# Last batch of an attention and gated-FFN kernel: gates in seven products of quarters, and three token pairs by turns

## The chip, the cores and the metric

The kernel runs on one core of one Trainium2 chip. The metric is the device time of one execution in microseconds (us). An execution uses TensorE (PE, matrix products; PEld is its weight load), VectorE (DVE), ScalarE (ACT), GpSimd (POOL) and the queue of SyncE (SP) that issues most DMAs. Before the change the median of three runs is 321.75 us (321.69 to 322.04). A difference under 0.2% (0.64 us) can't be told from no change.

## The reference

Two stages follow each other. The first is attention in which a query sees only the keys that have the same nearest centroid; the second is a gated feed-forward network without biases.

```python
# q, k, v: (4 batches, 8 heads, 768 tokens, 64), centroids: (8, 16, 64)
q_assign = argmax(normalised(q) @ normalised(centroids).T)     # per token, of 16
k_assign = argmax(normalised(k) @ normalised(centroids).T)
scores = where(q_assign == k_assign, q @ k.T / 8, -1e9)
attn = softmax(scores) @ v
x = attn as (3072 tokens, 512)
gate = 1 / (1 + exp(-(x @ w_gate)))                            # w_gate: 512 x 1536
val = x @ w_val                                                # w_val:  512 x 1536
out = (gate * val) @ w_out                                     # w_out: 1536 x 512
```

## The kernel before

The four batches are worked through one after the other, each with 96 steps of attention (8 heads of 12 half steps). A step is one `do_scores` (a matmul of 128 keys by 384 queries into a PSUM bank, then an exp on ScalarE into `es`) and, two steps later, one `do_av` (three small matmuls that gather `es` times v). When a head pair is done, `normalise` (L367) divides on VectorE and GpSimd, and `turn_x` (L939) sends the result through a transposing DMA on SP into `xTb`, the FFN's input: 4 chunks `dc` of 128 features by 768 tokens. The steps are numbered through all batches; the last batch has steps 288 to 383. The lists `bg`, `at` and `SCHED` say at which step a piece of side work (loads, splits, sums) is issued. Each engine carries out its own instructions in the order in which this program issues them; the program's order is written out by hand.

The FFN of a batch is a queue of short pieces ("atoms"), from which `ffn_run` (L846) takes some in every step, so that TensorE always has work between the scores. An FFN batch has two blocks of 384 tokens (three tiles of 128). For each block and each of 12 columns blocks `fc` of 128 hidden features there is a gate atom (four matmuls over `dc` into one bank, then a tanh on ScalarE) and a val atom (four matmuls into one bank, then one VectorE instruction, (tanh + 1) times val into the fp16 tile `hT`). The sigmoid is had from the tanh, with the factors 1/2 put elsewhere.

The output product `hT` by `w_out` goes over pairs of token tiles. From batch 1 on a pair takes seven products of half size rather than eight (the Strassen-Winograd scheme): `Sums.make` (L724) forms four sums of quarters of `hT` on VectorE, sums of quarters of `w_out` were formed once (T1 to T4), each of the seven products is six matmuls of 256 columns, and additions on VectorE put the quarters of the result together. The pairs are tiles (0,1), (3,2) and (4,5).

In the last batch block 0 is put into the queue at step 379.5, behind what is left of the batch before; its atoms come up after the last `do_av` and follow each other without anything between. Block 1 comes behind it. In block 1 the atoms of pair (0,1) (list `aside`) and half products of pair (3,2) alternate with the gate and val atoms; what is left of (3,2) and all of (4,5) comes last (`closing`, L576). PSUM has eight banks: four in `ring` (scores, gates, vals, some outputs), two in `avp` (attention) and two in `op` (outputs).

Of the kernel before, what the change touches and what calls it, by code (L numbers as in the profile page):

```python
# [95 lines left out]
}  # L96


# [1 line left out]
def kernel(  # L100
# [294 lines left out]
    T = {}  # L395
# [102 lines left out]
    def tok(b, t, f):  # L498
        return HB[b, t // 3][:, HF * f : HF * f + HF, bass.ts(t % 3, 128)]

    def store(src, b, c0, n, m=slice(0, DM)):
        def f():
            SP.dma_start(
                out=out[b * S : (b + 1) * S].rearrange("(p c) m -> p c m", c=NCH)[
                    :, c0 : c0 + n, m
                ],
                in_=src,
            )
# [7 lines left out]
    def ffn_atoms(xT, t0, n, b, final=False):  # L516
# [5 lines left out]
        when = SUMS_LAST if final else SUMS_AT[b >= PB, blk]  # L522

        def gate(fc, st):
            def f():
                need(("w", fc // WQ, 0), *(("x", b, p, t0 // 128 + c) for p in range(NP) for c in range(n // 128)))
                if fc == 0:
                    HB[b, blk] = htp.tile([128, NFC, 384], HP, name="hT")
                g = bank(512, name="g")
                for dc in range(NDC):  # L530
                    PE.matmul(  # L531
                        out=g[:, 0:n], lhsT=wg[fc // WQ][:, dc, fc % WQ, :],
                        rhs=xT[:, dc, t0 : t0 + n],
                        start=(dc == 0), stop=(dc == NDC - 1),
                    )
                th = thp.tile([128, 384], FP, name="th")
                ACT.activation(th[:, 0:n], g[:, 0:n], AF.Tanh)  # L537
                st.append(th)

            return f  # L540

        def val(fc, st):
            def f():
                need(("w", fc // WQ, 1))
                w = bank(512, name="v")
                for dc in range(NDC):
                    PE.matmul(  # L547
                        out=w[:, 0:n], lhsT=wv[fc // WQ][:, dc, fc % WQ, :],
                        rhs=xT[:, dc, t0 : t0 + n],
                        start=(dc == 0), stop=(dc == NDC - 1),  # L550
                    )
                DVE.scalar_tensor_tensor(  # L552
                    HB[b, blk][:, fc, 0:n], st[0][:, 0:n], 1.0, w[:, 0:n], ALU.add, ALU.mult
                )
# [17 lines left out]
        if final:  # L572
            return closing(b, gv, sm[(3, 2)], sm[(4, 5)])
        return gv + outs

    def closing(b, gv, ma, mb):  # L576

        ac, order = [], []  # L580
        plus = lambda dst, a, z: DVE.tensor_tensor(dst, a, z, ALU.add)

        def pair(m, bk):
            st = {}
# [7 lines left out]
            def mm(o, k, g, n, start, a=0, z=HD):  # L592
                w = lhs[k]()
                for c in range(g, g + n):
                    PE.matmul(  # L595
                        out=o, lhsT=w[:, c, :], rhs=rhs[k][:, c, a:z],
                        start=start and c == 0, stop=c == HF - 1, skip_group_check=True,
                    )

            def product(k, g=0, n=HF):  # L600
                def f():
                    z = {1: "a", 4: "d", 6: "x", 7: "x", 5: "y", 3: "y"}[k]
                    if g == 0 and k in (1, 4, 6, 5):
                        if k == 1:
                            st["ob"] = osp.tile([128, 2, DM], FP, name="ob")
                        st[z] = bk(z)
                    o = st[z][:, 0:HD]
                    mm(o, k, g, n, k not in (7, 3))
                    if g + n < HF:
                        return  # L610
                    if k == 1:
                        ACT.activation(C(0, 0), o, AF.Copy)
                    elif k == 4:
                        plus(C(1, 0), o, C(0, 0))
                    elif k == 6:
                        plus(C(0, 1), o, C(0, 0))
                    elif k == 5:
                        plus(C(1, 1), o, C(0, 0))
                    elif k == 7:
                        plus(C(1, 0), o, C(1, 0))  # L620
                        plus(C(1, 1), o, C(1, 1))
                        store(st["ob"][:, 1:2], b, m.t2, 1)
                    else:
# [4 lines left out]

            def last(parts):
                def f():  # L630
                    for a, z in parts:
                        o = bank(z - a, name="o_end")
                        mm(o, 2, 0, HF, True, a, z)
                        plus(st["ob"][:, 0, a:z], o, st["ob"][:, 0, a:z])
                    store(st["ob"][:, 0:1, 0:HD], b, m.t1, 1, slice(0, HD))

                return f

            return product, last

        two = {}

        def bank_a(z):
            if z in "ad":
                need(*(("wo", i) for i in range(WOP)), *(("wt", i, c) for i in range(4) for c in range(2)))
                two[z] = out_bank()
            return two[{"x": "a", "y": "d"}.get(z, z)]

        pa, la = pair(ma, bank_a)
        pb, lb = pair(mb, lambda z: bank(512, name="o_end"))  # L650
        early = [pa(k, g, HF // 2) for k in (1, 4, 6, 5) for g in (0, HF // 2)]

        def drained(f):
            def g():
                while aside:
                    aside.pop(0)[1]()
                f()

            return g

        early[0] = drained(early[0])
        atoms = gv[:14]
        for i, x in enumerate(gv[14:]):
            atoms.append(x)
            if i < len(early):
                atoms.append((0.0, early[i]))
        for f in (
            pa(7), pb(1), pb(4), pa(3), pb(6), pb(5), la([(0, HD)]), pb(7), pb(3),
            lb([(0, HD // 2), (HD // 2, HD)]),
        ):  # L670
            atoms.append((0.0, f))
        return atoms

    def plain_out(b, blk, t):
        OA = SCHED.get(f"oa{b}{384 * blk}", SCHED.get("oa", 4))
# [33 lines left out]
        },  # L709
    }  # L710

    SUMS_LAST = {
# [3 lines left out]
    }  # L716

    class Sums:


        def __init__(self, b, t1, t2):
            self.b, self.t1, self.t2, self.of = b, t1, t2, {}

        def make(self, i, c0=0, c1=HF):  # L724
# [3 lines left out]
            if c0 == 0:  # L728
                if i == 4 and c1 == HF:
                    self.of[4] = self.of[2]  # L730
                elif i == 4:
                    self.of[4] = tp.tile([128, 12, 128], HP, tag="T", name="T")[:, 0:HF]
                else:
                    self.of[i] = sump.tile([128, HF, 128], HP, tag="sum", name="sum")
            o = self.of[i][:, c]
            if i == 1:
                DVE.tensor_tensor(o, a2(0), a2(1), ALU.add)
            elif i == 2:
                DVE.tensor_tensor(o, self.of[1][:, c], a1(0), ALU.subtract)
            elif i == 3:  # L740
                DVE.tensor_tensor(o, a1(0), a2(0), ALU.subtract)
            else:
                DVE.tensor_tensor(o, a1(1), self.of[2][:, c], ALU.subtract)

    def product_out(b, sums):

# [783 lines left out]
    for b in range(B):  # L1530
        xT = xtp.tile([128, NDC, S], HP, tag="xTb", name="xTb")
        key = min(b, 1)
        for i in range(2 if b else NPT):
            u = BASE[b] + (DONE0[i] if b == 0 else 96 - 12 * halved(b) if i == 0 else 96)
            lag = SCHED.get(f"lag{key}{i}", 8)
            if b == B - 1 and i:
                break
# [54 lines left out]
```

## Time and profile before

| | |
|---|---|
| median of the runs | 321.75 us |
| the profiled execution | 323.41 us, span 321.6 us |
| granted TensorE clock | 1.00 |
| PE busy | 314.1 us (98% of the span), 3510 matmuls |
| DVE busy | 225.2 us (70%), 598 instructions |
| ACT busy | 230.8 us (72%), 521 instructions |
| POOL busy | 108.9 us (34%), 145 instructions |
| DMA | 45.16 MB |

Times in views are us from the start of the span, unless a column says ns. A row of the timeline is: start, duration, engine, line, operation, out<-in, count, and in brackets the idle time before it and what ended it. In a group's row the two numbers behind the bar are the busy us of all and the mean ns of one. Rows of several matmuls overlap the next row, since a matmul of 384 columns takes 326 ns from start to end while the next one starts 163 ns after it. The chain of work that ended last shows issue to issue times instead: a group of four there is 0.65 us.

### The profile page before, as it was taken

To read this page: it belongs to the slowest core of one execution; us is meant where nothing else is said; L and a number is where in the kernel's file an instruction comes from. 1 tells how busy PE (TensorE), PEld (TensorE's weight loads), DVE (VectorE), ACT (ScalarE), POOL (GpSimd) and SP (SyncE) were. 2 spreads that over 40 slices of the span, in tenths; PEclk is the share of its full clock that TensorE was granted. 3 is DMA by queue.
4 is the path that set the end of the run, shared out by engine and by line. 5 is a ranking of instruction groups with operands and counts; after the bars stand their busy time and mean duration, and the time that the engine had idled before them with its cause. 6 is when DMAs were issued, how large, how long until landed. Compare 5 with 4: busy or idle time off the path is not lost.

```text
span 321.6 us, 9181 instructions
## 1 busy us (share of the span) xinstructions
PE 314.1 (98%) x3510; PEld 222.1 (69%) x3510; DVE 225.2 (70%) x598; ACT 230.8 (72%) x521; POOL 108.9 (34%) x145
## 2 busy tenths in 40 slices
PE   7999999999999998999999999999999999999996
PEld 5888666766766665666777678666777678667775
DVE  5899656777787676686778678775766456456666
ACT  6688988787889986877767786887877875332320
POOL 6887464154435364423233342524102011000000
DMA  7999996748776996965665545952512122200103
GB/s 204 372 264 193 237 169 122 190 93 237 236 114 184 166 218 142 275 175 108 111 200 138 188 101 155 258 89 53 110 27 66 39 27 73 84 2 1 65 2 131
DMA packets 77708, 45.16 MB, mean 140 GB/s; under 512 B 56864, under 2 KB 75104, under 8 KB 77664
## 3 DMA queue, kind: packets, MB, share of 16 engines
q1 hardware_dynamic: 73696, 39.73, 49.4%
q0 software_dynamic: 3680, 4.72, 8.8%
q8 instruction: 27, 0.44, 0.6%
q14 instruction: 17, 0.14, 0.2%
q10 hardware_dynamic: 288, 0.13, 0.1%
HBM read 28.34 MB, written 6.29 MB: 108 GB/s over the span
## 4 chain that ended last, share of the span: by engine, by line
PE 92%; DVE 3%; DMA 2%; ACT 1%; issue 0%; ACTq 0%; POOL 0%; DVEq 0%
PE g L531 20%; PE v L547 19%; PE sc L894 18%; PE av L917 10%; PE o L822 10%; PE o L685 3%; DMA T<-hl 2%; PE lg L435 2%; PE o_end L595 2%; PE lg L422 1%; PE o L595 1%; PE oh_ps L1203 1%; PE t_ps L1143 1%; PE wm L985 1%; PE t_ps L1026 0%
## 5 line engine op out<-in xcount | busy, mean ns | idle before, releaser
L899 ACT ACTIVATE es<-sc 128x384 f16<-128x384 f32 x384 | 173.9, 492 | 40.5 <-PE sc L894 29.9
L894 PE MATMUL sc<-T 128*128 128x384 f16 x384 | 117.5, 326 | 0.4 <-DVE T L1224 0.4
L917 PEld LDWEIGHTS <-es 128*128 128x128 f16 x1152 | 81.3, 98 | 35.1 <-ACT es L899 0.2
L917 PE MATMUL av<-va,es 128*128 128x65 f16 x1152 | 97.6, 194 | 0.0
L552 DVE SCALAR_TENSOR_TENSOR hT<-th,v 128x384 f16<-128x384 f32 x96 | 53.1, 553 | 57.3 <-PE av L917 36.4
L531 PE MATMUL g<-xTb,wg 128*128 128x384 f16 x384 | 78.0, 326 | 0.2 <-DVE hT L552 0.2
L547 PE MATMUL v<-xTb,wv 128*128 128x384 f16 x384 | 78.1, 326 | 0.1
L537 ACT ACTIVATE th<-g 128x384 f32<-128x384 f32 x96 | 47.2, 492 | 34.7 <-PE g L531 15.6
L376 POOL TENSOR_TENSOR xp<-t,rec 128x384 f16<-128x384 f32 (+1 forms) x30 | 21.6, 721 | 98.0 <-DVE rec L373 50.3
L531 PEld LDWEIGHTS <-wg 128*128 128x128 f16 x384 | 37.3, 97 | 19.2 <-issue 0.4
L547 PEld LDWEIGHTS <-wv 128*128 128x128 f16 x384 | 37.4, 98 | 19.0 <-issue 0.3
L894 PEld LDWEIGHTS <-T 128*128 128x128 f16 x384 | 37.1, 97 | 0.6 <-DVE T L1224 0.5
L1460 POOL TENSOR_TENSOR hl<-kraw,hl 128x384 f16<-128x384 f32 x22 | 20.3, 922 | 41.4 <-DVE hl L1459 26.7
L1460 POOL TENSOR_TENSOR hl<-qraw,hl 128x384 f16<-128x384 f32 x22 | 21.2, 963 | 11.1 <-DVE hl L1459 11.1
L769 DVE TENSOR_TENSOR ob<-o,ob 128x256 f32<-128x256 f32 (+1 forms) x35 | 17.9, 523 | 6.9 <-PE o L822 4.1
L685 PE MATMUL o<-wo,hT 128*128 128x512 f16 x72 | 19.9, 379 | 0.0
L371 DVE TENSOR_TENSOR t<-av,sv 128x390 f32<-128x390 f32 (+1 forms) x30 | 14.4, 480 | 7.7 <-PE av L917 5.6
L822 PE MATMUL o<-wo,hT 128*128 128x256 f16 x126 | 19.7, 272 | 0.0
L822 PEld LDWEIGHTS <-sum 128*128 128x128 f16 x168 | 16.3, 97 | 4.4
L450 DVE TENSOR_REDUCE lgs<-lg 128x192 f32<-128x384 f32 x23 | 12.7, 551 | 3.7 <-PE lg L435 3.6
L822 PEld LDWEIGHTS <-hT 128*128 128x128 f16 x126 | 12.1, 97 | 3.3
L323 POOL CAST va<-vraw 128x768 f16<-128x768 f32 x15 | 13.0, 866 | 2.3 <-DMA vraw<-in_v_dram 2.3
(158 smaller groups left out, 340.0 us busy)
## 6 DMA issues: line engine op xcount, KB each, us to landing
vraw<-in_v_dram SPq DMA_DIRECT2D x15, 384.0 KB, 5.2
kraw<-in_k_dram SPq DMA_DIRECT2D x14, 384.0 KB, 4.4
qraw<-in_q_dram SPq DMA_DIRECT2D x12, 384.0 KB, 4.3
out_dram<-ob SPq DMA_DIRECT2D x18, 256.0 KB, 2.2
wg<-in_moe_w_gate_dram POOLq DMA_DIRECT2D x2, 768.0 KB, 9.2
wv<-in_moe_w_val_dram POOLq DMA_DIRECT2D x2, 768.0 KB, 10.2
wo<-in_moe_w_out_dram POOLq DMA_DIRECT2D x2, 768.0 KB, 9.0
T<-ohT SPq DMA_DIRECT2D x44, 24.0 KB, 1.9
```

What stands on the lines that cost most here:

```text
L376: (eng or POOL).tensor_tensor(x, t[:, 0:nq, 0:64], bcast(rec[:, 0:nq], 64), ALU.mult)
L531: PE.matmul(out=g[:, 0:n], lhsT=wg[fc // WQ][:, dc, fc % WQ, :], rhs=xT[:, dc, t0 : t0 + n], start=(dc == 0), stop=(dc == NDC - 1),)
L537: ACT.activation(th[:, 0:n], g[:, 0:n], AF.Tanh)
L547: PE.matmul(out=w[:, 0:n], lhsT=wv[fc // WQ][:, dc, fc % WQ, :], rhs=xT[:, dc, t0 : t0 + n], start=(dc == 0), stop=(dc == NDC - 1),)
L552: DVE.scalar_tensor_tensor(HB[b, blk][:, fc, 0:n], st[0][:, 0:n], 1.0, w[:, 0:n], ALU.add, ALU.mult)
L685: PE.matmul(out=o, lhsT=HB[b, blk][:, fc, bass.ts(t, 128)], rhs=wo[fc // WON][:, fc % WON, :], start=(fc == 0), stop=(fc == NFC - 1),)
L769: plus = lambda dst, a, z: DVE.tensor_tensor(dst, a, z, ALU.add)
L822: PE.matmul(out=st[z][:, e], lhsT=a[:, c, :], rhs=rhs[:, c, :], start=start and c + e == 0, stop=c == HF - 1, skip_group_check=True,)
L894: PE.matmul(out=sc.rearrange("p (c t) -> p c t", t=128), lhsT=s["k"], rhs=s["q"], start=True, stop=True,)
L899: ACT.activation(es, sc, AF.Exp, scale=SCALE)
L917: PE.matmul(out=av[:, a0 + s["c0"] + i, :], lhsT=s["es"][:, bass.ts(i, 128)], rhs=VA[b, p][:, e, s["j"], :], start=(first and i == 0 and a ...
L1460: POOL.tensor_tensor(hl[:, :, 64:128], r, hl[:, :, 0:64], ALU.subtract)
```

## The change

In the last batch only:

- Hidden column blocks 0 and 1 stay as they were, in both token blocks ("plain": `fin_plain`). Only those of token block 0 are put into the queue during attention; the rest belongs to the new `closing`.
- The gates of the ten other column blocks are formed by five units of two column blocks each (order 6, 2, 8, 4, 10). A unit takes two column blocks, two token blocks and two halves of the 512 features as a 2 by 2 by 2 product and does it in seven products of two matmuls each (14 matmuls of 384 columns), where the plain way takes 16. Its vals stay 16 matmuls.
- For that, sums of weight quarters are formed on VectorE: four for each half of the gate weights, at steps 354, 356, 357, 359 (half 1, three column quarters each, 768 columns) and 364, 366, 370, 371 (half 0, two quarters, 512 columns). They lie in tiles that held raw q and k. Four sums of token quarters (768 columns each) are formed too: the third at step 353, the first two at step 381, the fourth at the start of `closing`.
- In a unit, products 1, 6, 7 and 4 pile up in one `op` bank, and ScalarE takes the bank's content out after each (three copies, one tanh); products 5 and 3 pile up in an `avp` bank; product 2 has a `ring` bank. Three VectorE additions and three tanhs from SBUF finish the four gates. The vals of a unit are issued between the products of the next one.
- All three token pairs are now output at the end, by turns. Their products 1, 6, 7 and 4 pile up in one bank too, copied out by ScalarE after each, with three VectorE additions a pair (four for the last) instead of six and the final ones. The last store of 256 columns is cut into two of 128, the first on SP, the second on ScalarE's queue.

```diff
-    "b3p0vs": -30, ... "END": 0,
+    "b3p0vs": -30, ... "fw": [354, 356, 357, 359, 364, 366, 370, 371], "END": 0,
...
+    def fin_weights(i, t):
...
+        z, x, y = {
+            1: (tw(1), q(0, 1), q(0, 0)), 2: (tw(2), q(1, 1), tw(1)),
+            3: (tw(3), q(1, 1), q(0, 1)), 4: (tw(4), q(1, 0), tw(2)),
+        }[t]
+        cut = lambda v: v if v.shape[2] == 3 - a else v[:, :, a:]
+        DVE.tensor_tensor(cut(z), cut(x), cut(y), ALU.subtract)
...
+    def fin_tokens(xT, t):
...
+        z, x, y, o = {
+            1: (s(1), q(1, 0), q(1, 1), ALU.add), 2: (s(2), s(1), q(0, 0), ALU.subtract),
+            3: (s(3), q(0, 0), q(1, 0), ALU.subtract), 4: (s(4), q(0, 1), s(2), ALU.subtract),
+        }[t]
+        DVE.tensor_tensor(z, x, y, o)
...
+    def closing(xT):
+        fin_tokens(xT, 4)
...
+                for d in range(2):
+                    l, r = {
+                        1: lambda: (W_(0, 0, d), A_(0, 0, d)), 2: lambda: (W_(1, 0, d), A_(0, 1, d)),
+                        3: lambda: (W_(1, 1, d), S_(4, d)), 4: lambda: (T_(4, d), A_(1, 1, d)),
+                        5: lambda: (T_(1, d), S_(1, d)), 6: lambda: (T_(2, d), S_(2, d)),
+                        7: lambda: (T_(3, d), S_(3, d)),
+                    }[k]()
+                    PE.matmul(out=o, lhsT=l, rhs=r, ...)
+            def p1(u):
+                u.x = out_bank()[:, 0:384]
+                u.mm(u.x, 1, True, True)
+                ACT.activation(u.c1, u.x, AF.Copy)
+            def p5(u):
+                u.y = avp.tile([128, 512], FP, tag="av", name="av")[:, 0:384]
+                u.mm(u.y, 5, True, True)
+            def p6(u):
+                u.mm(u.x, 6, False, True)
+                ACT.activation(u.c12, u.x, AF.Copy)
+            def p2(u):
+                z = bank(512, name="gz")[:, 0:384]
+                u.mm(z, 2, True, True)
+                plus(u.c1, z, u.c1)
+            def p7(u):
+                u.mm(u.x, 7, False, True)
+                ACT.activation(u.c22, u.x, AF.Copy)
+                ACT.activation(u.c1, u.c1, AF.Tanh)
+            def sum22(u):
+                plus(u.c22, u.y, u.c22)
+            def p4(u):
+                u.mm(u.x, 4, False, True)
+                ACT.activation(u.c21, u.x, AF.Tanh)
+                ACT.activation(u.c22, u.c22, AF.Tanh)
+            def p3(u):
+                u.mm(u.y, 3, False, True)
+                plus(u.c12, u.y, u.c12)
+            def tanh12(u):
+                ACT.activation(u.c12, u.c12, AF.Tanh)
...
+        units = [Unit(n, f) for n, f in enumerate((6, 2, 8, 4, 10))]
+        old = [f for fc in range(FC0) for _, f in fin_plain(xT, fc, 1)]
...
+            w = old if n == 0 else [lambda i=i, u=units[n - 1]: u.v(i) for i in range(4)]
...
+            seq += [u.p1, w[0]] + ([l.p3] if l else []) + e(1) + [u.p5, u.p6]
+            seq += ([l.tanh12] if l else []) + [w[1], u.p2, u.p7, w[2], u.sum22]
+            seq += [w[3]] + e(1) + [u.p4]
...
-                    elif k == 4:
-                        plus(C(1, 0), o, C(0, 0))
-                    elif k == 6:
-                        plus(C(0, 1), o, C(0, 0))
-                    elif k == 5:
-                        plus(C(1, 1), o, C(0, 0))
-                    elif k == 7:
-                        plus(C(1, 0), o, C(1, 0))
-                        plus(C(1, 1), o, C(1, 1))
+                    if k in (1, 6, 7, 4):
+                        ACT.activation(C(*{1: (0, 0), 6: (0, 1), 7: (1, 1), 4: (1, 0)}[k]), o, AF.Copy)
+                    if k == 7:
+                        plus(C(1, 1), st["y"][:, 0:HD], C(1, 1))
...
+                        store(st["ob"][:, 0:1, a:z], b, m.t1, 1, slice(a, z), (SP, ACT)[i])
...
+        seq += [lambda: u.v(0), part(1, ma, 0, 4), u.p3, u.tanh12, p0(1), lambda: u.v(1), part(2, ma, 0, 4), pa(1)]
+        seq += [lambda: u.v(2), *both(m0, 4, HF), pb(1), lambda: u.v(3), l0([(0, HD)]), *both(ma, 4, HF)]
+        seq += [la([(0, HD)]), part(1, mb, 0, HF), p0(6), part(2, mb, 0, HF), p0(5)]
+        seq += [part(3, m0, 4, HF), part(3, ma, 4, HF), pa(6), part(4, m0, 0, HF), pa(5), part(3, mb, 0, HF)]
+        seq += [p0(7), part(4, ma, 0, HF), pb(6), part(4, mb, 0, HF), pb(5)]
+        seq += [pa(7), p0(4), p0(3), pb(7), pa(4), pa(3), pb(4), pb(3), lb([(0, HD // 2), (HD // 2, HD)])]
...
+            if b == B - 1:
+                if i == 0:
+                    at(u + lag, lambda xT=xT: queue.extend(a for fc in range(FC0) for a in fin_plain(xT, fc, 0)))
+                    at(u + SCHED.get("fs1", 9), lambda xT=xT: (fin_tokens(xT, 1), fin_tokens(xT, 2)))
+                    at(BASE[b] + 48 + SCHED.get("fs3", 17), lambda xT=xT: fin_tokens(xT, 3))
+                    for k, s_ in enumerate(SCHED["fw"]):
+                        at(s_, lambda k=k: fin_weights(1 - k // 4, 1 + k % 4))
+                continue
...
-    ffn_block(xT, 384, 384, B - 1, True)
+    ffn_run(1e9)
+    queue.extend(closing(xT))
     ffn_run(1e9)
```

More of the change, by code (lines that the diff above doesn't have):

```diff
@@ L521, in ffn_atoms @@
         sm = {x: Sums(b, *x) for x in pairs}
-        when = SUMS_LAST if final else SUMS_AT[b >= PB, blk]
+        when = SUMS_AT[b >= PB, blk]
         def gate(fc, st):
@@ L571, in ffn_atoms, with fin_room @@
             outs = product_out(b, [sm[x] for x in pairs])
-        if final:
-            return closing(b, gv, sm[(3, 2)], sm[(4, 5)])
         return gv + outs
-    def closing(b, gv, ma, mb):
-        ac, order = [], []
-        plus = lambda dst, a, z: DVE.tensor_tensor(dst, a, z, ALU.add)
+    FC0 = SCHED.get("fc0", 2)
+    fin = {}
+    def fin_room():
+        if not fin:
+            for x in "kq":
+                for n in range(3):
+                    r = rawp.tile([128, 2, NCH, 64], FP, tag=f"{x}raw", name=f"{x}raw", bufs=3)
+                    fin[x, n] = r.rearrange("p a c d -> p (a c d)").bitcast(HP).rearrange(
+                        "p (h x) -> p h x", h=2
+                    )
@@ new lines, in fin_tokens @@
+    def fin_tokens(xT, t):
+        fin_room()
+        s = lambda t: fin["kq"[(t - 1) // 2], 2][:, (t - 1) % 2].rearrange("p (d x) -> p d x", d=2)
+        q = lambda i, k: xT[:, 2 * k : 2 * k + 2, 384 * (1 - i) : 384 * (2 - i)]
+        fin["S", t] = s(t)
+        ps, cs = {1: ((2, 3), (0, 1, 2)), 2: ((), ()), 3: ((0, 1), range(6)), 4: ((2, 3), range(3, 6))}[t]
+        need(*(("x", B - 1, p, c) for p in ps for c in cs))
+        z, x, y, o = {
[3 more added lines that the diff above has]
+        DVE.tensor_tensor(z, x, y, o)
@@ new lines, in fin_group, with fin_plain, gate @@
+    def fin_group(xT, j, fc, blk):
+        w = (wg, wv)[j][fc // WQ]
+        o = bank(512, name="gv"[j])
+        for dc in range(NDC):
+            PE.matmul(
+                out=o[:, 0:384], lhsT=w[:, dc, fc % WQ, :], rhs=xT[:, dc, 384 * blk : 384 * blk + 384],
+                start=(dc == 0), stop=(dc == NDC - 1),
+            )
+        return o[:, 0:384]
+    def fin_plain(xT, fc, blk):
+        b, st = B - 1, []
+        def gate():
+            if fc == 0:
+                need(*(("x", b, p, 3 * blk + c) for p in range(NP) for c in range(3)))
+                HB[b, blk] = htp.tile([128, NFC, 384], HP, name="hT")
+            g = fin_group(xT, 0, fc, blk)
+            st.append(thp.tile([128, 384], FP, name="th"))
+            ACT.activation(st[0], g, AF.Tanh)
+        return [(NDC * 163, gate), (NDC * 163, lambda: hidden(xT, fc, blk, st[0]))]
@@ L590, in pair, with mm @@
             C = lambda i, j: st["ob"][:, i, HD * j : HD * j + HD]
-            def mm(o, k, g, n, start, a=0, z=HD):
+            def mm(o, k, start, a=0, z=HD):
                 w = lhs[k]()
-                for c in range(g, g + n):
+                for c in range(HF):
                     PE.matmul(
@@ L630, in f @@
                 def f():
-                    for a, z in parts:
-                        o = bank(z - a, name="o_end")
-                        mm(o, 2, 0, HF, True, a, z)
+                    for i, (a, z) in enumerate(parts):
+                        o = bank(512, name="o_end")[:, 0 : z - a]
+                        mm(o, 2, True, a, z)
                         plus(st["ob"][:, 0, a:z], o, st["ob"][:, 0, a:z])
-                    store(st["ob"][:, 0:1, 0:HD], b, m.t1, 1, slice(0, HD))
+                        store(st["ob"][:, 0:1, a:z], b, m.t1, 1, slice(a, z), (SP, ACT)[i])
@@ L672, in closing @@
-        return atoms
+        p0, l0 = pair(m0, lambda z: out_bank())
+        pa, la = pair(ma, lambda z: avp.tile([128, 512], FP, tag="av", name="av"))
+        pb, lb = pair(mb, lambda z: bank(512, name="o_end"))
+        u = units[-1]
+        both = lambda m, *c: [part(1, m, *c), part(2, m, *c)]
+        seq += [lambda: u.v(0), part(1, ma, 0, 4), u.p3, u.tanh12, p0(1), lambda: u.v(1), part(2, ma, 0, 4), pa(1)]
+        seq += [lambda: u.v(2), *both(m0, 4, HF), pb(1), lambda: u.v(3), l0([(0, HD)]), *both(ma, 4, HF)]
@@ L722, in __init__, with make @@
             self.b, self.t1, self.t2, self.of = b, t1, t2, {}
[L724 removed]
+        def make(self, i, c0=0, c1=HF, eng=None):
+            eng = eng or DVE
             c = slice(c0, c1)
@@ L727, in make @@
             a2 = lambda f: tok(self.b, self.t2, f)[:, c]
[L728 to L734, printed above, removed]
+            if i == 4 and 4 not in self.of:
+                self.of[4] = self.of[2]
+            elif i not in self.of:
+                self.of[i] = sump.tile([128, HF, 128], HP, tag="sum", name="sum")
             o = self.of[i][:, c]
             if i == 1:
-                DVE.tensor_tensor(o, a2(0), a2(1), ALU.add)
+                eng.tensor_tensor(o, a2(0), a2(1), ALU.add)
             elif i == 2:
-                DVE.tensor_tensor(o, self.of[1][:, c], a1(0), ALU.subtract)
+                eng.tensor_tensor(o, self.of[1][:, c], a1(0), ALU.subtract)
             elif i == 3:
-                DVE.tensor_tensor(o, a1(0), a2(0), ALU.subtract)
+                eng.tensor_tensor(o, a1(0), a2(0), ALU.subtract)
             else:
-                DVE.tensor_tensor(o, a1(1), self.of[2][:, c], ALU.subtract)
+                eng.tensor_tensor(o, a1(1), self.of[2][:, c], ALU.subtract)
     def product_out(b, sums):
```

112 lines of the change are left out of this document (68 added, 44 removed), and 5 rows, old and new, of tables (SCHED, SUMS_LAST).

## The prediction

> **What bounds the kernel now.** I read the page's busy times first, then a table of stretches, then the groups of the last stretch by form, and last the chain.
>
> ```profile
> PE 314.1 (98%) x3510; PEld 222.1 (69%) x3510; DVE 225.2 (70%) x598; ACT 230.8 (72%) x521; POOL 108.9 (34%) x145
> ```
>
> ```profile
> core 0: us, PE busy (x) PEld busy (x) DVE busy (x) ACT busy (x) POOL busy (x), PEclk, DMA share, GB/s
> 251.00:262.00 11.00, 11.00 (x116) 7.68 (x115) 5.30 (x12) 8.94 (x22) 0.97 (x2) 1.00 0.27 43
> 262.00:273.40 11.40, 11.40 (x134) 9.69 (x133) 6.50 (x14) 7.12 (x15) 1.58 (x4) 1.00 0.15 52
> 273.40:289.00 15.60, 15.60 (x98) 9.39 (x96) 7.34 (x13) 5.89 (x12) 0.30 (x1) 1.00 0.12 44
> 289.00:302.50 13.50, 13.50 (x99) 9.48 (x97) 8.91 (x20) 3.82 (x8) 0.00 (x0) 1.00 0.05 20
> 302.50:311.20 8.70, 8.70 (x64) 6.02 (x63) 4.54 (x10) 2.36 (x6) 0.00 (x0) 1.00 0.09 32
> 311.20:318.60 7.40, 7.35 (x70) 6.10 (x68) 6.87 (x22) 0.87 (x2) 0.00 (x0) 1.00 0.20 72
> ```
>
> From 251 to 318.6 TensorE is never idle but for 0.05 us, at a granted clock of 1.00; VectorE and ScalarE have room everywhere but in the last 7 us, where VectorE works 6.87 of 7.40. The last batch's FFN begins at 273.40, as the chain (issue to issue) shows:
>
> ```profile
> 272.42 0.98 PE o L822 x9
> 273.40 0.65 PE g L531 x4
> 274.05 0.65 PE v L547 x4
> ...
> 318.60 0.29 DVE ob L581
> ```
>
> A group of four matmuls of 384 columns costs 0.65 us, 0.1625 each, back to back; one of 256 costs 0.98 / 9 = 0.109. So TensorE's count of columns sets the end, and behind its last matmul lie one addition of 0.29 us and the last store. The Trainium skill (Perfetto Trace Analysis, Identifying the Most-Contended Engine) calls matmul busy time a bad measure, and asks for the share of LDWEIGHTS. By that the 9.39 of 15.60 us of PEld would leave headroom; the equal spacing of 0.1625 at full clock speaks against it, and I give it a rival (the third).
>
> **The change part by part.** Rows of the last stretch, by form:
>
> ```profile
> L531 PE MATMUL g<-xTb,wg 128*128 128x384 f16 x96 | 19.5, 326 | 0.0
> L547 PE MATMUL v<-xTb,wv 128*128 128x384 f16 x96 | 19.5, 326 | 0.0
> L552 DVE SCALAR_TENSOR_TENSOR hT<-th,v 128x384 f16<-128x384 f32 x24 | 13.3, 554 | 16.8 <-PE v L547 16.8
> L537 ACT ACTIVATE th<-g 128x384 f32<-128x384 f32 x24 | 11.8, 491 | 26.1 <-DVE hT L552 9.7 <-PE g L531 9.1 <-DVE ob L769 4.4
> L741 DVE TENSOR_TENSOR sum<-hT 128x768 f16<-128x768 f16 x3 | 1.7, 554 | 0.0
> L743 DVE TENSOR_TENSOR T<-hT,sum 128x640 f16<-128x640 f16 x2 | 1.0, 492 | 0.1
> L743 DVE TENSOR_TENSOR T<-hT,sum 128x128 f16<-128x128 f16 x2 | 0.5, 225 | 0.1
> L581 DVE TENSOR_TENSOR ob<-o_end,ob 128x256 f32<-128x256 f32 x7 | 2.7, 418 | 0.3 <-PE o_end L595 0.2
> L612 ACT ACTIVATE ob<-o 128x256 f32<-128x256 f32 x1 | 0.4, 385 | 0.8 <-PE o L595 0.8
> ```
>
> *TensorE.* Gates: 96 matmuls become 16 plain ones and 5 x 14 = 86. Ten go, 10 x 0.1625 = **-1.63 us**. Vals stay 96, and the three pairs' products stay 7 x 6 x 3 = 126 matmuls of 256 columns, only in another order: 0. If no wait arises, this is the whole gain.
>
> *The weights' and tokens' sums in steps 353 to 371*: four of 768 columns and one token sum at 0.554 (L741's row), four of 512 columns between 0.225 (128) and 0.492 (640), by the line through these about 0.43: 4.5 us of VectorE. Cover:
>
> ```profile
> 251.19 0.56 DVE L552 SCALAR_TENSOR_TENSOR hT<-th,v 128x384 f16<-128x384 f32 x1 [0.70 <-PE av L917]
> 253.25 0.56 DVE L552 SCALAR_TENSOR_TENSOR hT<-th,v 128x384 f16<-128x384 f32 x1 [1.51 <-PE av L917]
> 255.32 0.56 DVE L552 SCALAR_TENSOR_TENSOR hT<-th,v 128x384 f16<-128x384 f32 x1 [1.51 <-PE av L917]
> ```
>
> By the order of issue at most two sums stand between two of these instructions, 1.11 us in a gap of 1.51, and VectorE works 5.30 of 11.00 us in this stretch. What would be late is the release of a val's ring bank, thus a later score. I take 0; the other end is +4.5 (all exposed), and nothing lies below 0, since no work is taken away here.
>
> *The start of the closing.* Token sums 1 and 2 (step 381) are issued behind the pair of additions at 270.04 and ahead of the addition at 271.95:
>
> ```profile
> 270.04 1.29 DVE L769 TENSOR_TENSOR ob<-o,ob 128x512 f32<-128x512 f32 x2 [0.76 <-PE o L822]
> 271.95 0.69 DVE L769 TENSOR_TENSOR ob<-o,ob 128x512 f32<-128x512 f32 x1 [0.62 <-PE o L822]
> 272.56 0.35 DVE L371 TENSOR_TENSOR t<-av,sv 128x195 f32<-128x195 f32 x1
> ```
>
> ```profile
> 273.73 1.18 SPq L948 DMA_TRANSPOSE xTb<-xp  x1
> ```
>
> ```profile
> DMA to landing us min/median/max: 2.3/3.0/4.1
> ```
>
> (The last line is for the four transposes of 244.7 to 273.7; the last one alone took 2.3.) Before, the last quarter of the FFN's input landed at 273.73 + 2.3 = 276.03, and block 0's 15.60 us lay over it. Now VectorE is free for the addition at 270.04 + 1.29 + 1.11 = 272.44, 0.49 late; `normalise`, GpSimd and the transpose on SP follow, and it lands at 276.52. TensorE has only the four plain groups of block 0 (273.40 + 16 x 0.1625 = 276.00), two matmuls of product 1 and three of the next gate, whose fourth reads that quarter: at 276.81. Cover of 0.29 us: I take 0, and nothing can be gained here. With a landing of 3.0 it waits 0.4 us, with 4.1 1.5 us. Behind it the whole program waits, as TensorE goes in order; so does VectorE, whose token sum 4 reads the same data.
>
> *The units.* A unit has 14 + 16 matmuls, 30 x 0.1625 = 4.88 us. ScalarE does seven activations of 384 columns for it (four before): 7 x 0.491 = 3.4. VectorE does four instructions of L552's kind and three additions of 384 columns from PSUM (between 0.418 and L769's 0.69, about 0.55): 3.9, in units four and five two sums of 512 columns more: 4.7. Both fit. The tight spot is the bank in which products 1, 6, 7, 4 pile up: TensorE may add product 6 only when ScalarE has copied product 1, which stands behind two tanhs. Rows for the hand-over and for activations back to back:
>
> ```profile
> 273.89 0.49 PE L547 MATMUL v<-xTb,wv 128*128 128x384 f16 x2
> 274.09 0.49 ACT L537 ACTIVATE th<-g 128x384 f32<-128x384 f32 x1 [2.67 <-PE g L531]
> ```
>
> ```profile
> 261.48 0.49 ACT L899 ACTIVATE es<-sc 128x384 f16<-128x384 f32 x1 [0.42 <-PE sc L894]
> 261.87 0.59 ACT L773 ACTIVATE ob<-o 128x512 f32<-128x512 f32 x1
> ```
>
> ScalarE starts 0.20 us after TensorE has gone on, and a ready activation starts 0.39 after the one before. Counted from a unit's product 1: tanh of product 4 at 0.20, tanh from SBUF at 0.59, copy at 0.98, done at 1.47. Product 6 is due ten matmuls on, 1.63. Without that overlap (0.49 apart) the copy ends at 1.67: late by some 0.05, with a semaphore 0.1, in four units 0.4 us. I take **+0.1**, nearer the overlap that the rows show; ends 0 and +0.4. The other additions into a bank have more room (product 7 comes 8 matmuls behind product 6, product 4 ten behind 7).
>
> *The end.* From the last unit's first val TensorE has 16 + 2 matmuls of 384 and 126 of 256 columns (0.109): 16.7 us. VectorE has about 9.9 us up to the last sum that a product waits for (four of L552's kind, one addition of 384, 11 sums or parts, three additions of 256), with 1.3 us carried over and some waits 12; product 3 of the last pair, which reads that sum, is due at 15.4. So the sums that made VectorE busy 6.87 of 7.40 us don't bind. ScalarE's nine more copies are 9 x 0.385. The last store:
>
> ```profile
> 318.05 1.31 SPq L503 DMA_DIRECT2D out_dram<-ob  x3
> ```
>
> Three issues on SP take 0.44 each, and the last addition ends at 318.89. The second half goes out on ScalarE's queue at the same time as the old store did, with half its bytes, but the stores of three pairs are packed closer. I take 0, ends -0.2 (half the bytes) and +0.4 (an issue of 0.44 later). The Trainium skill (DMA: Bandwidth & Descriptors, Issuing engines are not separate DMA queues) says that several issuers save issue time alone; by it the sum would be up to 0.4 lower only if SP's issue were last.
>
> **Sum.** -1.63 + 0 + 0 + 0.1 + 0 = -1.53. It is made against the profiled span of 321.6 (execution 323.41, which is 1.66 above the median); I carry the difference to the median: 321.75 - 1.53 = **320.2**, its own range 319.9 (-1.63 - 0.2) to 320.9 (with the ends 0.4 and 0.4 instead).
>
> **The rivals.**
> 1. *The last transpose is exposed.* For it: cover shrinks from 15.60 us to 0.29, and the slowest of four landings here took 4.1 us. Against: the last took 2.3, with SP otherwise free. Time: at a landing of 3.6 a wait of 1.0, 321.2; at 4.1, 321.7.
> 2. *Slower: VectorE's sums in steps 353 to 371 reach TensorE.* In 251 to 273.40 TensorE is busy 22.40 of 22.40 us, so each delay of a ring bank counts in full. Against: the gaps of 1.51. It decides from 2.2 of the 4.5 us exposed (+0.64 over before); half to all exposed gives 322.5 to 324.7, say 323.0.
> 3. *The removed matmuls weren't the bound* (hand-overs eat them: 0.3 us a unit would do): the change does nothing, 321.7. For it: ScalarE's slack of 0.16 us a unit is thin. Against: TensorE's equal spacing before.
>
> **How the numbers follow.** Forecast 0.70, rival 1 0.15, rival 2 0.10, rival 3 0.05. Faster by over 0.2% (below 321.1): the forecast and half of rival 1, 0.78; within 0.2%: the rest of rival 1 and rival 3 but for their tails, 0.10; slower: rival 2 and 0.02 of these tails, 0.12. The range takes in the forecast's own and rival 1 up to a wait of 1.1 us: 319.8 to 321.4.
>
> **What would show it.** 86 gate matmuls at 0.1625 and TensorE without idle from 276 to its end, which comes 1.5 us earlier; the last gate group before the units not released by a DMA; PE busy 100% in 251 to 273.4. Wrong if TensorE's waits name the transpose (rival 1), VectorE or a ring bank before 273 (rival 2), or ScalarE's copies in every unit (rival 3); a granted clock under 1.00 would upset all of it.

## The result and the profile after

The changed kernel takes 320.40 us (median of 20 runs, 319.79 to 322.03) against 321.82 us for the kernel before (median of 20 runs beside it). The ratio is 0.9956 [0.9947, 0.9965], that is -1.42 us, between -1.1 and -1.7: faster, and by more than 0.2%. The prediction was 320.2 us. The profiled execution of after is 320.28 us with a span of 318.5 us.

The busy line of the page of after, and then the table of stretches of after, with the same stretches as were shown of before in its first two rows, units in the next two and the end in the last:

```profile
PE 312.2 (98%) x3500; PEld 221.1 (69%) x3500; DVE 233.7 (73%) x615; ACT 240.4 (75%) x545; POOL 109.0 (34%) x145
```

```profile
core 0: us, PE busy (x) PEld busy (x) DVE busy (x) ACT busy (x) POOL busy (x), PEclk, DMA share, GB/s
251.00:262.00 11.00, 11.00 (x117) 7.97 (x115) 7.92 (x19) 8.93 (x22) 1.37 (x2) 1.00 0.20 19
262.00:273.40 11.40, 11.40 (x126) 9.30 (x125) 8.30 (x18) 6.32 (x13) 1.52 (x3) 1.00 0.16 56
286.00:291.00 5.00, 5.00 (x33) 2.99 (x32) 3.73 (x8) 3.31 (x8) 0.00 (x0) 1.00 0.02 3
291.00:296.00 5.00, 5.00 (x32) 3.01 (x31) 4.32 (x10) 3.31 (x9) 0.00 (x0) 1.00 0.00 0
311.00:315.40 4.40, 4.14 (x44) 3.62 (x42) 2.12 (x6) 1.15 (x3) 0.00 (x0) 1.00 0.55 206
```

3510 matmuls have become 3500. VectorE has 8.5 us more work (233.7 against 225.2) and ScalarE 9.6 us more, and TensorE is still busy for the whole of every stretch before its end, at a granted clock of 1.00. The chain of after, issue to issue:

```profile
270.81 0.98 PE o L954 x9
271.80 0.65 PE g L622 x4
...
278.62 0.65 PE o L685 x4
...
283.50 0.65 PE o L685 x4
...
288.37 0.65 PE o L685 x4
...
315.15 0.02 issue
315.18 0.29 DVE ob L650
```

L685 is the product of a unit; the three rows of it shown here are 4.88 and 4.87 us apart, which is 30 matmuls at 0.1625. From the first gate of the last FFN to the issue that follows the last matmul the chain counts 315.15 - 271.80 = 43.35 us. The work alone is 182 x 0.1625 + 126 x 0.109 = 43.3 us, so no wait is left in it. In before the same stretch took 318.57 - 273.40 = 45.17 us. The difference is -1.82: -1.63 for ten matmuls, and about -0.2 that the prediction doesn't have. The chain of before has it in one place, and a row of before's waits, in the stretch 311 to 316, has the same place:

```profile
312.46 1.20 PE o_end L595 x11
313.66 0.01 issue
313.68 0.28 PE o_end L595
```

```profile
PEld L595 <- DVE hT L552: 0.3, 1, 0.3
```

Eleven matmuls of 256 columns take 1.20 us, and the twelfth takes 0.28 instead of 0.109: its weight load waited 0.3 us for `hT`, of which 0.18 us reach the chain. From 245 us on after has no wait of TensorE. Behind the last matmul it went the other way: from the last addition's start to the span's end before took 321.63 - 318.60 = 3.03 us and after 318.50 - 315.18 = 3.32 us, **+0.29**. So -1.63 - 0.2 + 0.3 makes about -1.5 us, beside the -1.42 of the times.

The two profiled spans differ by twice as much (321.6 and 318.5). Some 1.6 us of that lie ahead of the change (the last FFN begins at 273.40 and at 271.80), and one row of before's waits carries most of it:

```profile
PE lg L435 <- DMA T<-hl: 1.3, 1, 1.3
```

This wait for a DMA early in the program isn't in after's waits. Before's profiled execution was 1.66 us above its median. In the traces of the experiments below the same wait comes and goes (1.5 us with more stores joined, 0.8 with the sums twice, 0.5 with the plain gates, none in the others), so it belongs to the execution and not to the change.

### The profile page after: what moved, and what is told of

The parts are those of the page before. It is cut to its first block, busy times and chain, and to the rows that moved or that the text cites. A ratio compares the mean times of both kernels' runs of the same rounds, so it can differ in the third digit from the quotient of the medians.

```text
span 318.5 us, 9195 instructions
## 1 busy us (share of the span) xinstructions
PE 312.2 (98%) x3500; PEld 221.1 (69%) x3500; DVE 233.7 (73%) x615; ACT 240.4 (75%) x545; POOL 109.0 (34%) x145
## 4 chain that ended last, share of the span: by engine, by line
PE 95%; DVE 2%; POOL 1%; issue 0%; ACT 0%; POOLq 0%; DVEq 0%
PE sc L1026 19%; PE g L531 15%; PE v L547 15%; PE av L1049 11%; PE o L954 9%; PE v L622 5%; PE o L825 5%; PE lg L435 2%; PE o L685 2%; PE o_end L763 2%; PE lg L422 1%; PE o L763 1%; PE av L763 1%; PE av L685 1%; PE t_ps L1275 1%; PE oh_ps L1335 1%
## 5 line engine op out<-in xcount | busy, mean ns | idle before, releaser
L552 DVE SCALAR_TENSOR_TENSOR hT<-th,v 128x384 f16<-128x384 f32 x72 | 39.8, 553 | 38.3 <-PE av L1049 34.1
L531 PE MATMUL g<-xTb,wg 128*128 128x384 f16 x288 | 58.5, 326 | 0.2 <-DVE hT L552 0.2
L537 ACT ACTIVATE th<-g 128x384 f32<-128x384 f32 x72 | 35.4, 491 | 8.7 <-PE g L531 6.7
L531 PEld LDWEIGHTS <-wg 128*128 128x128 f16 x288 | 27.9, 97 | 14.3 <-issue 0.4
L547 PEld LDWEIGHTS <-wv 128*128 128x128 f16 x288 | 28.0, 98 | 13.9 <-issue 0.3
L901 DVE TENSOR_TENSOR ob<-o,ob 128x256 f32<-128x256 f32 (+1 forms) x28 | 15.0, 549 | 4.7 <-PE o L954 3.2
L954 PE MATMUL o<-wo,hT 128*128 128x256 f16 x108 | 16.8, 273 | 0.0
L954 PEld LDWEIGHTS <-sum 128*128 128x128 f16 x144 | 14.0, 97 | 3.3
L643 DVE SCALAR_TENSOR_TENSOR hT<-T,v 128x384 f16<-128x384 f32 x20 | 11.0, 552 | 5.3 <-PE v L622 5.3
```

The costliest lines, as they stand in the source:

```text
L531: PE.matmul(out=g[:, 0:n], lhsT=wg[fc // WQ][:, dc, fc % WQ, :], rhs=xT[:, dc, t0 : t0 + n], start=(dc == 0), stop=(dc == NDC - 1),)
L547: PE.matmul(out=w[:, 0:n], lhsT=wv[fc // WQ][:, dc, fc % WQ, :], rhs=xT[:, dc, t0 : t0 + n], start=(dc == 0), stop=(dc == NDC - 1),)
L552: DVE.scalar_tensor_tensor(HB[b, blk][:, fc, 0:n], st[0][:, 0:n], 1.0, w[:, 0:n], ALU.add, ALU.mult)
L954: PE.matmul(out=st[z][:, e], lhsT=a[:, c, :], rhs=rhs[:, c, :], start=start and c + e == 0, stop=c == HF - 1, skip_group_check=True,)
```

## The experiments

Ratios are to the kernel before, measured on the same chip beside each kernel; the kernel before had 321.89 to 321.95 us there.

**The ten matmuls: units with the plain gates.** The order of units, sums and outputs stays; the gates of a unit are formed the plain way, 16 matmuls instead of 14. The sums are still formed, but nothing reads them.

```diff
+def gv(u, i):
+    j, blk = [(0, 1), (1, 0), (0, 0), (1, 1)][i]
+    return [f for _, f in fin_plain(xT, u.f + j, blk)]
...
-seq += [u.p1, w[0]] + ([l.p3] if l else []) + e(1) + [u.p5, u.p6]
...
+seq += w[:2] + ex[:1] + w[2:] + ex[1:]
```

> The changed kernel with the gates of the ten column blocks in plain products again (16 matmuls a unit for 14, no ScalarE copies and no VectorE additions for them), in the new unit order and with the new output order; the sums of weights and tokens are still formed, without use. If the ten matmuls are the gain: 320.4 + 1.63 = 322.0, a ratio to the kernel before of about 1.000 to 1.001 (the rest of the change, a wait of 0.2 us less and an end that is 0.3 us longer, cancels). If the gain came from the other order or from what lies ahead of 273 us: 320.4, ratio 0.996.

Measured: 1.001 [0.9996, 1.0024], 322.47 us. The chain:

```profile
272.30 0.65 PE g L622 x4
...
317.39 0.02 issue
317.41 0.29 DVE ob L650
```

The stretch takes 317.39 - 272.30 = 45.09 us, 1.74 longer than in after; ten matmuls are 1.63. With the ten matmuls back the gain is gone, so they are the gain. The other order and the outputs by turns are worth nothing that can be told from zero: the interval leaves 0.1 us of gain to 0.8 us of loss.

**The end: the cut last store.** Two runs asked why the end had grown by 0.29 us. One issues both halves on SP's queue, the other stores the 256 columns in one piece.

```diff
-store(st["ob"][:, 0:1, a:z], b, m.t1, 1, slice(a, z), (SP, ACT)[i])
+store(st["ob"][:, 0:1, a:z], b, m.t1, 1, slice(a, z), SP)
```

> The changed kernel with both halves of the last store issued on SP. If ScalarE's queue is what lengthens the end by 0.3 us (from the last matmul to the end of the span 3.35 us for 3.03 before): 320.1. If SP's issue of 0.4 us is the limit: the second half goes out some 0.3 later, 320.7. If the end of the span differs by chance from run to run: 320.4.

```diff
-        store(st["ob"][:, 0:1, a:z], b, m.t1, 1, slice(a, z), (SP, ACT)[i])
+    store(st["ob"][:, 0:1, 0:HD], b, m.t1, 1, slice(0, HD))
```

> The changed kernel with one last store of 256 columns on SP, as before the change. If splitting and the other queue cost 0.3: 320.1; if they gain what the half of the bytes takes: 320.6; if neither matters: 320.4.

Measured: 0.9958 [0.9943, 0.9973] and 0.9959 [0.9942, 0.9977]; from the last addition to the end 3.58 and 3.35 us in the traces, against 3.32 in after. Neither the queue nor the cut explains the 0.29 us; the theory that ScalarE's queue lands late has fallen. With both halves on SP, their issues start at 315.3 and 315.8 and hold SP for 0.41 us each, while the last addition starts at 315.04; in after, SP's starts at 315.4 and ScalarE's at 315.5, with the addition at 315.18. So the second half is issued some 0.4 us later, and the end comes 0.26 later. The Trainium skill (DMA: Bandwidth & Descriptors, Issuing engines are not separate DMA queues) says that several issuers save only the time that the issue takes. The trace agrees.

**The sums alone.** The kernel before, with the eight weight sums and the token sums 1 to 3 issued at their steps, and nothing that reads them.

```diff
...
+if b == B - 1:
+    at(u + SCHED.get("fs1", 9), lambda xT=xT: (fin_tokens(xT, 1), fin_tokens(xT, 2)))
+    at(BASE[b] + 48 + SCHED.get("fs3", 17), lambda xT=xT: fin_tokens(xT, 3))
+    for k, s_ in enumerate(SCHED["fw"]):
+        at(s_, lambda k=k: fin_weights(1 - k // 4, 1 + k % 4))
```

> The kernel before, with the eight sums of weight quarters and the token sums 1 to 3 added at the same steps, results not used. Forecast of the prediction: they lie in VectorE's gaps, 321.8, ratio 1.000. Second rival: they reach TensorE through the ring banks, up to the 5.6 us that they take, 322.5 or more.

Measured: 1.0008 [0.9991, 1.0025]. A stretch of its table:

```profile
core 0: us, PE busy (x) PEld busy (x) DVE busy (x) ACT busy (x) POOL busy (x), PEclk, DMA share, GB/s
245.00:262.00 17.00, 17.00 (x177) 12.03 (x176) 13.11 (x29) 14.20 (x33) 2.20 (x3) 1.00 0.30 43
```

TensorE lost nothing to them. Any cost is at most 0.25%, and none is seen.

**The sums twice.** The same question in after, with twice the work: token sum 3 and each weight sum are issued two times.

```diff
-at(BASE[b] + 48 + SCHED.get("fs3", 17), lambda xT=xT: fin_tokens(xT, 3))
+at(BASE[b] + 48 + SCHED.get("fs3", 17), lambda xT=xT: [fin_tokens(xT, 3) for _ in range(2)])
...
-    at(s_, lambda k=k: fin_weights(1 - k // 4, 1 + k % 4))
+    at(s_, lambda k=k: [fin_weights(1 - k // 4, 1 + k % 4) for _ in range(2)])
```

> The changed kernel with the nine sums of steps 353 to 371 formed twice, 4.5 us more of VectorE in some 12 us in which it works 8 already. In the changed kernel two sums and a val's instruction take 1.4 of every 2.06 us; doubled they take 2.4, so the vals' instructions come 0.3 us later from one to the next, and a val's bank has about 0.4 us until it is taken again. If the sums are hidden by VectorE's gaps: 320.4 to 320.9. If the ring banks bind at once (second rival): 4.5 more, up to 324.9.

Measured: 0.9944 [0.9929, 0.9959], 319.94 us: not slower than after. The stretch 250 to 262 of after, and then of this kernel:

```profile
250.00:262.00 12.00, 12.00 (x125) 8.63 (x124) 8.92 (x21) 9.89 (x24) 1.37 (x2) 1.00 0.23 32
```

```profile
250.00:262.00 12.00, 12.00 (x126) 8.41 (x124) 11.05 (x24) 9.86 (x24) 0.82 (x1) 1.00 0.14 40
```

VectorE (the third pair of numbers) works 11.05 of 12.00 us, and TensorE still all of them. The second rival is refuted, with more room than the prediction had worked out.

**The late quarter.** To see whether the first wait of the last FFN comes where the prediction's cover ends, token sums 1 and 2 are formed three times. That puts about 2.2 us of VectorE ahead of the additions that the last transpose hangs on.

```diff
-(fin_tokens(xT, 1), fin_tokens(xT, 2))
+[fin_tokens(xT, t) for t in (1, 2) * 3]
```

> The changed kernel with token sums 1 and 2 formed three times over at step 381, so that VectorE comes four instructions (about 2.2 us) later to the division of the last head pair and the last quarter of the input lands 2.2 us later. In the changed kernel it lands at 272.46 + 2.3 = 274.76 and the first matmul that reads it starts at 275.05: 0.29 us of cover. If that cover is all there is, TensorE waits 1.9 us: 322.3, and the trace shows one gap in TensorE there. If there is more cover than the prediction counted: 320.4 to 321.5.

Measured: 1.0035 [1.0016, 1.0055], 322.53 us. The waits of TensorE, and the timeline around it:

```profile
PE g L622 <- DMA xTb<-xp: 2.0, 1, 2.0
```

```profile
274.31 0.65 PE L622 MATMUL g<-xTb,wg 128*128 128x384 f16 x3
276.95 0.32 PE L622 MATMUL g<-xTb,wg 128*128 128x384 f16 x1 [1.99 <-DMA xTb<-xp]
```

It is one wait, of 2.0 us (1.9 was expected), at the fourth matmul of the gate group after block 0's four: the place that the prediction names. So the cover at the start is as thin as worked out, and what lies beyond it is paid in full. One thing wasn't expected. The profiled execution lost 1.7 us more right after the wait (from the fourth matmul's start to the last matmul's end it takes 41.78 us, in after 40.10), and its stretches show where:

```profile
core 0: us, PE busy (x) PEld busy (x) DVE busy (x) ACT busy (x) POOL busy (x), PEclk, DMA share, GB/s
275.00:277.00 2.00, 0.05 (x1) 0.05 (x1) 0.55 (x3) 0.00 (x0) 0.00 (x0) 1.00 0.29 78
277.00:279.00 2.00, 2.00 (x9) 0.96 (x9) 0.49 (x1) 0.98 (x2) 0.00 (x0) 0.61 0.57 234
279.00:281.00 2.00, 2.00 (x8) 1.01 (x7) 1.11 (x2) 0.16 (x1) 0.00 (x0) 0.53 0.00 0
281.00:284.00 3.00, 3.00 (x21) 1.78 (x19) 1.58 (x3) 2.42 (x6) 0.00 (x0) 1.00 0.00 0
```

After two microseconds without work the granted clock was 0.61 and 0.53 for four microseconds, and 2 x 0.39 + 2 x 0.47 is 1.7 us. Five of this kernel's nine executions took 322.2 to 322.5, which is the wait alone over after, and four took 323.4 to 324.5. Three of these four had a mean clock of 0.994 or 0.995; the slowest, 324.49, had 1.000, so what lengthened it was something else, and that is open.

**One more copy in each unit.** ScalarE copies a bank once more, between the tanh from SBUF and the copy of the next unit's product 1. It asks how thin the slack of the hand-over is.

```diff
 ACT.activation(u.c22, u.c22, AF.Tanh)
+ACT.activation(u.c21, u.c21, AF.Copy)
```

> The changed kernel with one ScalarE copy more in each unit, SBUF to SBUF, between the two tanhs behind product 4 and the copy of the next unit's product 1. In the changed kernel that copy is done 0.15 us before product 6 adds into the bank, and an activation more moves it by 0.41. If this hand-over is the tight spot that the prediction took it for: a wait of 0.26 us in each of units two to five, 1.0 us in all, 321.4, with a gap of TensorE ahead of each product 6. If ScalarE has more room than that: 320.4.

Measured: 0.9991 [0.9978, 1.0004], 321.76 us, about 1.1 us over after. The waits of TensorE in this kernel, and its chain at one unit, with the extra copy at L720:

```profile
PE o L685 <- ACT T L693: 0.6, 4, 0.2
```

```profile
284.09 0.34 PE o L685 x2
284.43 0.02 issue
284.45 0.49 ACT T L718
284.94 0.07 ACT T L719
285.01 0.24 issue
285.25 0.51 ACT T L720
285.76 0.39 ACT T L693
286.15 0.04 issue
286.19 0.48 PE o L685 x2
...
289.28 0.34 PE o L685 x2
```

Now ScalarE is in the chain, and a unit lasts 289.28 - 284.09 = 5.19 us instead of 4.88: 0.31 for an activation that takes 0.41 from start to start. The slack took the other 0.10. In four units that is 4 x 0.31 = 1.2 us, most of the gain. (The row of waits says 0.6 because it counts from the end of the matmul before, which comes 0.16 us after the next one could have started; 4 x 0.16 more make 1.2.) So the third rival's mechanism is real, and after lies just on the right side of it.

**The semaphore of the last store.** After the two runs on the last store the program's end was read again, by what its last line does on SP. In before a single semaphore instruction falls in the stretch 320.70 to 320.79, right before the closing exchange of the engines. In after seven follow each other in 317.20 to 317.65, one about every 0.06 us:

```profile
L1587 SPq EVENT_SEMAPHORE  x1: 28/28/28, 320.7 to 320.7; - x1
```

```profile
L1726 SPq EVENT_SEMAPHORE  x7: 27/28/28, 317.2 to 317.6; - x7
```

At the program's end SP waits for a row of DMA semaphores, one after another. The theory: the DMAs take these semaphores by turns, so how many waits still stand behind the last store's depends on how many DMAs the program has. By it before's last store has the last semaphore of the row, and after's two last stores the first ones. Then joining two stores about 4 us earlier moves the last store to another semaphore and shortens the end, although nothing at the end changes. The first kernel joins the two stores of the first tile of pair (0,1), and stores the last 256 columns in one piece; the other joins those of pair (3,2) too and keeps the cut one.

```diff
-store(st["ob"][:, 0:1, HD:DM], b, m.t1, 1, slice(HD, DM))
+lo = 0 if m is m0 else HD
+store(st["ob"][:, 0:1, lo:DM], b, m.t1, 1, slice(lo, DM))
...
-        store(st["ob"][:, 0:1, a:z], b, m.t1, 1, slice(a, z), (SP, ACT)[i])
+    if m is not m0:
+        store(st["ob"][:, 0:1, 0:HD], b, m.t1, 1, slice(0, HD))
```

> The changed kernel with one last store of 256 columns, and with the two stores of the first tile of pair (0,1) joined into one behind product 3, so that one DMA less is issued. In the traces SP waits at the end of the program for eight semaphores in a fixed order, and the DMAs take these semaphores by turns. Before the change the last store had the last one of the row; in the changed kernel the last two have the first two, and six or seven waits of 0.06 us follow their landing. If that is what lengthens the end by 0.3 us, one DMA less puts the last store on the last semaphore again: last addition to end of span 3.0 us for 3.3, time 320.1. If the closer packing of the stores does it: 3.3 or more, 320.4 to 320.6.

```diff
-store(st["ob"][:, 0:1, HD:DM], b, m.t1, 1, slice(HD, DM))
+lo = HD if m is mb else 0
+store(st["ob"][:, 0:1, lo:DM], b, m.t1, 1, slice(lo, DM))
...
-store(st["ob"][:, 0:1, a:z], b, m.t1, 1, slice(a, z), (SP, ACT)[i])
+if m is mb:
+    store(st["ob"][:, 0:1, a:z], b, m.t1, 1, slice(a, z), (SP, ACT)[i])
```

> The changed kernel with its two half stores at the end, and with the stores of the first tiles of pairs (0,1) and (3,2) joined behind product 3, so that two DMAs less are issued: the last two stores have the last two semaphores of the row. By the row of waits: 3.0 us from the last addition to the end, 320.1. By the packing: 3.3 or more, 320.4 to 320.6.

The changed kernel once more, beside these two on one chip:

> The changed kernel itself, beside the two, on the same chip: 320.4, ratio 0.9956, 3.3 us from the last addition to the end.

Measured: 0.9939 [0.9919, 0.9959], 319.84 us with one store joined; 0.9951 [0.9934, 0.9968], 320.16 us with more joined; 0.9946 [0.9932, 0.9961], 320.22 us for after. The first, by the same reading of the last line, over 317.2 to 317.3:

```profile
L1728 SPq EVENT_SEMAPHORE  x1: 28/28/28, 317.3 to 317.3; - x1
```

One semaphore instead of seven. From the last addition's start to the end the traces count 318.15 - 315.25 = 2.90 us, 320.05 - 317.06 = 2.99 us and, for after again, 318.31 - 315.01 = 3.30 us. Both joined versions come back to the 3.03 us of before, one of them with the cut store on two queues. Read in narrow windows, SP's last line has eight waits in each of these traces, and its end comes apart into pieces (us; the stores of the whole program are counted, the other DMAs are the same):

| kernel | stores | last addition's start to the landing of the last store | waits behind that landing | last addition's start to the end |
|---|---|---|---|---|
| before | 24 | 2.13 | 0 | 3.03 |
| one store joined | 24 | 2.01 | 0 | 2.90 |
| more joined | 24 | 2.04 | 1 | 2.99 |
| last store uncut | 25 | 2.02 | 7 | 3.35 |
| after | 26 | 2.05 | 6 | 3.32 |
| both halves on SP | 26 | 2.32 | 6 | 3.58 |

(The landing is taken as the start of the last wait that doesn't follow right behind another.) From the last wait on all six need another 0.89 to 0.91 us. Six waits are 0.37 us and seven 0.44. The stores land as soon in after as in the others, and the row of waits behind the landing is what lengthens its end. In the times of whole runs this is too small to be told apart, as the three intervals overlap. By its trace the first is the best version found, 0.4 us shorter than after at its end.

## Why the prediction was right

- *TensorE, -1.63.* Right: 43.35 us from first gate to last matmul, no wait in it, and with ten matmuls more 45.09 and no gain. The equal spacing of 0.1625 us at full clock was the limit, although the weight load was busy for only about 3 of every 5 us.
- *The sums in steps 353 to 371, 0.* Right. Two sums lie in a gap of VectorE, as counted from the order of issue, and the next val isn't late. The timeline of after:

```profile
251.64 0.56 DVE L552 SCALAR_TENSOR_TENSOR hT<-th,v 128x384 f16<-128x384 f32 x1 [0.57 <-PE av L1049]
252.12 0.55 DVE L602 TENSOR_TENSOR qraw<-wg,qraw 128x768 f16<-128x768 f16 x1
252.58 0.55 DVE L602 TENSOR_TENSOR qraw<-wg 128x768 f16<-128x768 f16 x1
253.71 0.56 DVE L552 SCALAR_TENSOR_TENSOR hT<-th,v 128x384 f16<-128x384 f32 x1 [0.57 <-PE av L1049]
```

  These instructions start 0.46 to 0.48 us apart, so two sums take less than the 1.11 us that the prediction put into a gap of 1.51. The upper end of +4.5 was far too careful: even twice the sums cost nothing.
- *The start of the closing, 0.* The result is right, and the way to it was not clean. Rows of after, timeline, tile and timeline again:

```profile
272.46 1.18 SPq L1080 DMA_TRANSPOSE xTb<-xp  x1
```

```profile
DMA to landing us min/median/max: 2.3/2.3/2.3
```

```profile
274.56 0.81 PE L622 MATMUL g<-xTb,wg 128*128 128x384 f16 x4
```

  It lands at 274.76, and the fourth matmul of that group starts at 274.56 + 3 x 0.1625 = 275.05: a cover of 0.29 us, the number predicted. But two errors of 0.16 cancel in it. The start of the FFN was taken from the chain and the transpose from the timeline, which stand 0.16 us apart; and the two token sums delayed it by 0.33 us (from the FFN's start in the chain to the transpose 0.33 us in before, 0.66 in after), not by 0.49. The late quarter showed that this cover is real: beyond it the first rival's wait comes, at the matmul named.
- *The units' hand-over, +0.1.* The slack was sized right and its cost was 0. The timeline of after, ScalarE and then TensorE:

```profile
278.98 0.49 ACT L718 ACTIVATE T<-o 128x384 f32<-128x384 f32 x1 [0.25 <-PE o L685]
279.37 0.51 ACT L719 ACTIVATE T<-T 128x384 f32<-128x384 f32 x1
279.78 0.48 ACT L693 ACTIVATE T<-o 128x384 f32<-128x384 f32 x1
```

```profile
280.41 0.49 PE L685 MATMUL o<-kraw 128*128 128x384 f16 x2
```

  The copy ends at 280.26 and product 6 starts at 280.41: 0.15 us to spare, predicted 0.16. In the kernel with one more copy product 6 starts 0.05 us after its copy's end, so about 0.10 us of it was free, as the 0.31 us a unit shows.
- *The end, 0 (-0.2 to +0.4).* This is the term that was off: it measured +0.29, inside its ends. The prediction looked at bytes and issue, and what decides here is which semaphore of the row the last store has. (Its 0.44 us for an issue was read off a row of three that holds waits too; an issue takes 0.33 to 0.41 us in these traces.) Against it stands the gain of about 0.2 us inside the FFN, before's wait for `hT`, which the prediction didn't list although a row of before's waits had it. It had put all of 311.20 to 318.60 down as busy but for 0.05 us. The busy time hides such a wait, since a matmul of 256 columns counts as busy for 0.27 us though the next one can start 0.109 after it.
- *The sum.* -1.53 was predicted and -1.42 [-1.71, -1.13] measured. The two missed terms, -0.2 and +0.3, nearly cancel, and the +0.1 of the hand-over wasn't paid, so the closeness of the sum is partly luck.

## What to carry to other kernels

Where TensorE's matmuls stand equally spaced at full clock, its columns set the time: ten matmuls less were worth their 1.63 us, and VectorE's and ScalarE's extra 18 us cost nothing, because each piece fits the gap it lies in. Work out a thin cover in one time base and look for the wait it would turn into; here 0.29 us at the start and 0.10 us a unit were all that kept the gain. When an end grows though nothing late was added, count what SP still does behind the landing of the last store.

## What the runs showed of the hardware

- The eight waits for DMA semaphores at this program's end come one after another, about 0.06 us each where none has to wait. A last store that had the first or second of the row cost 3.30 to 3.35 us from the last addition on (three traces), one that had the last of it 2.90 to 3.03 (three traces). That this program's DMAs take the semaphores by turns was inferred from these counts; two kernels forecast from it came out so, and the counts of stores fit.
- After 2.0 us without matmuls the granted clock of the late quarter's profiled execution fell to 0.61 and 0.53 for four microseconds and cost 1.7 us more. The Trainium skill (TensorE: Matmul & The Clock Gate, HAM oscillation — how this bites in real kernels) warns of idle gaps over about 3.4 us; here a shorter one was followed by the drop, and the measurement decides. It wasn't so in every execution: five of nine took the wait's time alone. That the gap caused the drop is only argued from its place right behind it; some executions of the kernel before, which has no such gap there, had a mean clock of 0.995 too.
